# An order planned with table loads and GpSimd's hold counted, exponentials of blocks 4 to 7 from PSUM, weights' signs by a relu's slope

## The chip, the core and the metric

One core of one Trainium2 chip runs the whole program. The metric is the device time of one execution in microseconds, median of three runs: 699.13 us (697.25 to 700.21).

## What is computed

Sliding-window attention, then a gated MLP, then an MLP with a normalised hidden layer, all in float32:

```
scores = (q @ k.T) / 8, kept where 0 <= i - j < 64       # 4 batches, 8 heads, 576 positions, 64 wide
x  = softmax(scores) @ v                                  # heads side by side: 2304 tokens x 512
h  = x @ w_in;   g = h * tanh(softplus(h));   x2 = g @ w_out              # 512 -> 2048 -> 512
h  = x2 @ w_in2; y = h * softmax(h);  z = (y - mean) / sqrt(var + 1e-6) * g_ln
out = z @ w_out2                                          # 512 -> 1024 -> 512
```

The weights come as 64-bit floats and are read as pairs of 32-bit words.

## The kernel before

Every matmul of the MLPs runs on split operands: a value is rounded to its high part, the rest is its low part, and three products (low by high, high by low, high by high) are summed in PSUM.

**Blocks and groups.** The 2304 tokens are 36 blocks of 64, in five groups of 512, 512, 512, 384 and 384 tokens. Blocks 0 to 3 (`attend_first`) go one by one, all others in pairs (`attend`, n = 4, 6, ...). A block's chain is: scores on PE (`a_qk`, L610; for blocks 0 to 7 the mask is added by a matmul, L595, L602), maximum on VectorE (`a_max`, L657), subtraction (`a_sub`, L667 or L670), exponential on ScalarE, sum, reciprocal (`a_norm`, L686), multiplication by it on VectorE or POOL (`a_mul`, L693), transposes on PE (`a_tr`, L705), eviction (`a_pt`, L308), product with v (`a_pv`, L742), and x with its high part (`a_x`) and low part (`a_xl`, L764). The pairs' scores, transposes and products share one PSUM tile of pool `ps_a`. Exponentials come in three forms: head by head from PSUM for blocks 0 to 3 (`a_exp0`, L627), in one instruction after `a_sub` (`a_exp`, L674: blocks 4 to 7 and from 16 on), and head by head in SBUF (`a_exp1`, L641: blocks 8 to 15).

**The mish loop.** `its` lists 84 steps: group 0 in two halves of 256 tokens for features 0 to 3, then whole groups. A step is `pe_m1` (L788, 12 matmuls), mish on ScalarE (`act_m`, L798), the high part g on either engine (`g_h`), the low part on VectorE (`g_l`, L316), `pe_m2` (L822, 8 matmuls) and `pe_m2l` (L833, 4). The attention of a group runs beside the mish steps of the group ahead.

**Weights.** A piece is loaded by SP (`c_load`, L354), then `c_up` (upper word, scaled by 2^-112), `c_low` (lower word as an integer, scaled), `c_bits` (both joined, L377), `c_sign` (the sign bit of the upper word added, L383), and the high and low parts (`c_hi`, `c_lo`).

**The last stage** multiplies pairs of tiles by w_in2 in seven products (`b_p`, L957), sums them (`b_c`), normalises, transposes (`b_tr`, L1040), splits the result into lz (`b_hi`, `b_lo`), and multiplies by w_out2 (`b_m4`, L1065).

**What sets the order.** Each instruction belongs to a step with a cost for each engine that may run it, a due time and its predecessors. `Schedule.run` places the steps one after the other on the engines by these costs and the rings of buffers, and issues them in that order; each engine then runs its own queue in order. The due times come from the constants at the top (`ATT_AT`, `MISH_AT`, ...). Where the planner leaves PE idle for over 0.8 us, `bridge` fills part of the wait with zero matmuls of 256 columns (L562), and `warm_up` begins with `N_WARM` of them. ScalarE's functions need a table to be loaded (ACT_TABLE_LOAD) when it goes from exponentials to mish or back; the copy needs none. The planner charges each exponential of blocks 8 to 15 for a table load, whether one is needed or not:

```
ex = step(dict(act=1.68 + 1.33), t + offs[4], a_exp1, n, range(NP), after=[su], uses=[s])
```

Of the kernel before, what the change touches and what calls it, by code (L numbers as in the profile page):

```python
# [24 lines left out]
P = 128  # L25
BLK = 64
# [7 lines left out]
EARLY = 2  # L34
COSTS = {
    "up1": {"act": 0.58, "pool": 0.7}, "up2": {"act": 1.05}, "low1": {"pool": 0.83, "act": 0.58}, "low2": {"act": 1.05},
# [6 lines left out]
    "mul0": {"pool": 1.05, "dve": 0.69}, "mul": {"pool": 2.2, "dve": 1.23},  # L43
# [34 lines left out]
N_WARM = 42  # L78
# [3 lines left out]
W_AT = -57.813  # L82
# [8 lines left out]
class Schedule:  # L91
# [11 lines left out]
    def step(self, costs, due, fn, *args, after=(), new=(), uses=()):  # L103

        s = Step()
        s.costs, s.due, s.fn, s.args, s.after, s.new = costs, due, fn, args, list(after), new
        s.end = s.engine = None
        for b in uses:
            b["users"].append(s)
        self.steps.append(s)  # L110
        return s

    def issue(self, s, t):
        self.idle = s.idle if s.engine == "pe" else 0.0
        if any(s.costs is c for c in COSTS.values()):
            s.fn(s.engine, *s.args)
        else:
            s.fn(*s.args)

    def run(self, sizes):  # L120
# [8 lines left out]
        free = {e: 0.0 for s in self.steps for e in s.costs}  # L129
        ready = {e: [] for e in free}  # L130
# [35 lines left out]
        while left:  # L166
# [21 lines left out]
            s.end = t + s.costs[e]  # L188
# [15 lines left out]
def attention_moe_solu(  # L204
# [34 lines left out]
    NM = GROUPS[0] // BLK if PE_MASK else N0  # L239
    assert GROUPS[0] // BLK <= NBB  # L240
# [391 lines left out]


# [28 lines left out]
    def a_sub(n):  # L662
        s, nm = s_t[n]
        nm = nm.unsqueeze(2).to_broadcast([P, 2 * NP, P])
        if n < NM:
            ps, s = s, at_p.tile([P, 2 * NP, P], F32, tag="s2", name="s", bufs=2)
            nc.vector.scalar_tensor_tensor(out=s, in0=ps, scalar=scale, in1=nm, op0=ALU.mult, op1=ALU.add)  # L667
            s_t[n] = s, nm
        else:
# [810 lines left out]
```

## Time and profile before

| | |
|---|---|
| median of the runs | 699.13 us (697.25 to 700.21) |
| the profiled execution | 698.97 us, its span 697.2 us |
| PE | 680.7 us busy (98%), 4373 matmuls |
| VectorE | 398.3 us (57%), 689 instructions |
| ScalarE | 363.7 us (52%), 612 instructions, 35 of them table loads |
| POOL | 49.1 us (7%), 68 instructions |
| granted clock of PE | 0.999 |

The span runs from the first to the last instruction on the core; the time is that of the whole execution. Busy time of PE counts zero matmuls too. Shares over the whole span mix stages with different limits, so the rows below are cut by stage.

### The profile page before, as it was taken

How to read it: one execution, taken by the hardware profiler on the slowest of the kernel's cores; microseconds unless marked ns; L12 is line 12 of the kernel's file. 1: busy time of each engine (PE TensorE's matmuls, PEld its weight loads, DVE VectorE, ACT ScalarE, POOL GpSimd, SP SyncE). 2: the span in 40 equal slices, each digit the busy share in tenths (PEclk: the TensorE clock that was granted, in tenths of full speed). 3: DMA queues.
4: the chain of work that ended last, by engine and by line, in shares of the span. 5: the costliest groups of instructions: out<-in, count | busy, mean ns of one | idle time of the engine just before them, and what ended most of it. 6: DMA issues, size and time to landing. Idle time of an engine off the chain costs nothing.

```text
span 697.2 us, 10836 instructions
## 1 busy us (share of the span) xinstructions
PE 680.7 (98%) x4373; PEld 584.7 (84%) x4373; DVE 398.3 (57%) x689; ACT 363.7 (52%) x612; POOL 49.1 (7%) x68
## 2 busy tenths in 40 slices
PE   9979899999999999999999999999999999999997
PEld 7778778888887878888889999999778888888886
DVE  4897777788355557411344134764688777775430
ACT  4769975658245454422254223663567566555431
POOL 4121100000011111000010000000011101110000
PEclk9999999999999999999999999999999999999999
DMA  8857246487046324200023003320211111100011
GB/s 286 304 179 275 92 152 214 149 307 236 7 152 206 122 91 151 91 1 0 1 92 121 1 1 106 132 80 25 81 47 47 45 46 61 61 31 15 16 47 45
DMA packets 37858, 71.74 MB, mean 103 GB/s; under 512 B 2864, under 2 KB 15152, under 8 KB 37808
## 3 DMA queue, kind: packets, MB, share of 16 engines
q1 hardware_dynamic: 37808, 71.06, 30.1%
q8 instruction: 34, 0.56, 0.3%
q14 instruction: 16, 0.13, 0.1%
HBM read 59.51 MB, written 11.53 MB: 102 GB/s over the span
## 4 chain that ended last, share of the span: by engine, by line
PE 88%; ACT 6%; DVE 2%; DMA 1%; issue 1%; SPq 0%; POOL 0%; ACTq 0%; POOLq 0%
PE ps_h L788 26%; PE x L822 18%; PE po L1065 14%; PE pb L957 11%; PE x L833 9%; PE pt L1040 2%; PE ps_s L610 2%; PE ps_o L742 2%; PE ps_t L705 2%; DMA st<-w_out 1%; PE ps_w L562 1%; ACT s L641 1%; ACT L641 1%; ACT L798 1%; ACT st L362 1%
## 5 line engine op out<-in xcount | busy, mean ns | idle before, releaser
L788 PE MATMUL ps_h<-xt,w 128*128 128x512 f32 (+2 forms) x1008 | 211.6, 359 | 0.0
L788 PEld LDWEIGHTS ps_h<-xt,w 128*128 128x128 f32 x1008 | 177.9, 188 | 21.7 <-issue 0.5
L822 PE MATMUL x<-g,w 128*128 128x512 f32 (+2 forms) x672 | 147.7, 361 | 1.0 <-ACT g L296 1.0
L822 PEld LDWEIGHTS x<-g,w 128*128 128x128 f32 x672 | 118.0, 188 | 15.3 <-ACT g L296 1.2
L316 DVE SCALAR_TENSOR_TENSOR g<-mc,g 128x512 fp32r<-128x512 f32 (+2 forms) x84 | 53.4, 636 | 125.5 <-ACT g L296 124.6
L798 ACT ACTIVATE mc<-ps_h 128x512 f32<-128x512 f32 (+2 forms) x84 | 44.8, 536 | 133.9 <-PE ps_h L788 132.2
L1065 PE MATMUL po<-w,lz 128*128 128x512 f32 x432 | 100.5, 390 | 0.7 <-ACT lz L1046 0.7
L1065 PEld LDWEIGHTS po<-w,lz 128*128 128x128 f32 x432 | 80.7, 188 | 17.6 <-ACT lz L1046 0.9
L833 PE MATMUL x<-g,w 128*128 128x512 f32 (+2 forms) x336 | 82.0, 365 | 0.0
L833 PEld LDWEIGHTS x<-g,w 128*128 128x128 f32 x336 | 58.7, 188 | 7.7 <-issue 1.2
L957 PE MATMUL pb<-w,xs 128*128 128x512 f32 x210 | 50.9, 398 | 0.0
L296 ACT ACTIVATE g<-mc 128x512 fp32r<-128x512 f32 (+2 forms) x61 | 35.0, 576 | 28.0 <-PE x L833 26.8
L957 PEld LDWEIGHTS pb<-w,xs 128*128 128x128 f32 x210 | 38.9, 188 | 8.9
L693 POOL TENSOR_TENSOR s<-s,rs 128x1024 f32<-128x1024 f32 x11 | 20.9, 1898 | 317.5 <-DVE rs L687 306.5
L957 PE MATMUL pb<-w,xs_w 128*128 128x512 f32 x168 | 40.4, 394 | 0.6 <-ACT v_b L308 0.6
L308 ACT ACTIVATE v_b<-pb 128x512 f32<-128x512 f32 x34 | 20.2, 597 | 34.5 <-PE pb L957 34.5
L1050 DVE TENSOR_TENSOR lz<-pt,lz 128x512 fp32r<-128x512 f32 x36 | 23.4, 686 | 24.9 <-ACT lz L1046 24.9
L957 PEld LDWEIGHTS pb<-w,xs_w 128*128 128x128 f32 x168 | 31.0, 188 | 7.3 <-ACT v_b L308 1.1
L377 DVE SCALAR_TENSOR_TENSOR st<-st 128x1024 uint32<-128x1024 uint32 x22 | 26.9, 1223 | 9.4 <-ACT st L369 8.1
L798 ACT ACT_TABLE_LOAD x17 | 21.8, 1283 | 16.6 <-PE ps_h L788 16.4
L1020 POOL TENSOR_SCALAR va<-va 128x1 f32<-128x1 f32 x18 | 9.8, 546 | 289.1 <-DVE va L1013 289.1
L1072 ACT ACTIVATE o<-po 128x512 f32<-128x512 f32 x18 | 10.8, 601 | 35.7 <-PE po L1065 22.4
(130 smaller groups left out, 781.7 us busy)
## 6 DMA issues: line engine op xcount, KB each, us to landing
qk<-qk SPq DMA_DIRECT2D x32, 512.0 KB, 4.8
st<-w_out SPq DMA_DIRECT2D x12, 1024.0 KB, 5.4
st<-w_in SPq DMA_DIRECT2D x10, 1024.0 KB, 6.0
v<-v SPq DMA_DIRECT2D x32, 256.0 KB, 3.5
xr<-x2d SPq DMA_DIRECT2D x18, 256.0 KB, 3.3
out<-o SPq DMA_DIRECT2D x18, 256.0 KB, 2.0
x2d<-xs SPq DMA_DIRECT2D x12, 256.0 KB, 3.9
part<-xs SPq DMA_DIRECT2D x8, 256.0 KB, 3.6
```

What stands on the lines that cost most here:

```text
L296: nc.scalar.activation(out=hi, in_=x, func=ACTF.Copy, scale=1.0 if g is None else g)
L308: nc.scalar.activation(out=out, in_=x, func=ACTF.Copy)
L316: nc.vector.scalar_tensor_tensor(out=lo, in0=x, scalar=1.0 if g is None else g, in1=hi.bitcast(F32), op0=ALU.mult, op1=ALU.subtract)
L377: nc.vector.scalar_tensor_tensor(out=lw, in0=uw, scalar=3, in1=lw, op0=ALU.logical_shift_left, op1=ALU.bitwise_or)
L693: eng.tensor_tensor(out=s, in0=s, in1=rs.to_broadcast(list(s.shape)), op=ALU.mult)
L788: nc.tensor.matmul(out=ps[:, :n], lhsT=w[:, a, k, fs], rhs=x[:, b, k, a0:a1], start=(idx == 0), stop=(idx == len(terms) - 1),)
L798: nc.scalar.activation(out=c[:, :n], in_=ht.pop(i)[:, :n], func=ACTF.Mish)
L822: nc.tensor.matmul(out=acc[j][m][:, a0:a1], lhsT=w[:, a, f % 4, m * P:(m + 1) * P], rhs=g[:, 0, :n], start=(i in opens and a == 0), stop=F ...
L833: nc.tensor.matmul(out=acc[j][m][:, a0:a1], lhsT=w[:, 0, f % 4, m * P:(m + 1) * P], rhs=g[:, 1, :n], start=False, stop=i in closes,)
L957: nc.tensor.matmul(out=ps, lhsT=x[:, a, ix, k, :], rhs=w[:, k, :], start=first and n == 0, stop=n == len(terms) - 1, skip_group_check=not ...
L1050: nc.vector.tensor_tensor(out=lt[t][:, 1, fs], in0=pst[t][:, fs], in1=lt[t][:, 0, fs].bitcast(F32), op=ALU.subtract)
L1065: nc.tensor.matmul(out=po[t], lhsT=lz[:, a, f, :], rhs=wt["w4", f // 4][:, b, f % 4, :], start=(c == 0 and idx == 0), stop=(c == 2 and idx ...
```

## The change

The planner keeps the table that ScalarE has loaded, and adds 1.3 us where a step needs the other one; it holds VectorE back while a POOL instruction of two operands runs; it counts the first matmuls at half rate, and starts with the DMAs. The costs of the exponentials lose their fixed table load. All due times have new values, so nearly every queue has a new order.

Blocks 4 to 7 (`NM` stays 8) no longer run `a_sub`: the new `a_exp2` takes each head's exponential from PSUM with scale and bias, and sums it on the way. The PSUM tile is free only after the eighth.

Where ScalarE has the exponentials' table at `c_up`, it runs a Prelu with slope 2^32 for negative values in place of the copy, and `c_sign` is dropped for that piece. The exponentials' rows of blocks 0 to 3 get a room of their own, with four slots in place of three (`N_S`). `N_WARM` goes from 42 to 30.

```
-    "mul0": {"pool": 1.05, "dve": 0.69}, "mul": {"pool": 2.2, "dve": 1.23},
+    "mul0": {"pool": 1.05, "dve": 0.69}, "mul": {"pool": 1.9, "dve": 1.23},
...
-ATT_AT = (-49.865, -54.03, 11.767, 61.451, 29.509, -54.936, 25.627, -16.828, 25.86, -58.794, 5.065, -38.341)
+ATT_AT = (-86.017, -45.412, -6.323, 72.547, -11.313, 2.222, 41.979, -34.721, 27.367, -76.85, -34.655, -4.363)
...
-N_WARM = 42
+N_S = 4
+N_MASKED = 8
+N_WARM = 30
...
+            if e == "act" and s.table and s.table != self.table:
+                return max(t, free[e] + LOAD)
             return max(t, free[e])
...
-            s.end = t + s.costs[e]
+            cost = s.costs[e]
+            if e == "pe" and t < COLD:
+                cost += min(cost, (COLD - t) / 2)
+            if s.table and e == "act":
+                self.table = s.table
+            if s.sign is not None and e == "act" and self.table == "exp":
+                s.sign.costs = COSTS["no_sign"]
+            if s.two and e == "dve":
+                a, b = max(t, shared[0]), shared[1]
+                if a < b and t + cost > a:
+                    cost += min(b - a, (t + cost - a) / 0.2) * 0.8
+            if s.two and e == "pool":
+                shared = t, t + cost
+                b = min(free["dve"], t + cost)
+                if b > t:
+                    free["dve"] += 0.8 * (b - t)
+            s.end = t + cost
...
         if e == "act":
-            nc.scalar.activation(out=w, in_=w, func=ACTF.Copy, scale=2.0**-112)
+            if sch.table == "exp":
+
+                nc.scalar.activation(out=w, in_=w, func=ACTF.Prelu, scale=2.0**-112, alpha=2.0**32)
+            else:
+                nc.scalar.activation(out=w, in_=w, func=ACTF.Copy, scale=2.0**-112)
...
+    def a_exp2(n, ps):
+        if 0 in ps:
+            s = at_p.tile([P, 2 * NP, P], F32, tag="s2", name="s", bufs=2)
+            s_t[n] = s, s_t[n][1], sm_p.tile([P, 2 * NP], F32, tag="su2", name="su"), s_t[n][0]
+        s, nm, su, w = s_t[n]
+        for p in ps:
+            nc.scalar.activation(
+                out=s[:, p], in_=w[:, p], func=ACTF.Exp, scale=scale, bias=nm[:, p:p + 1], accum_out=su[:, p:p + 1]
+            )
+        if 2 * NP - 1 in ps:
+            s_t[n] = s, nm, su
...
-                su = step(dict(dve=1.23), t + offs[3], a_sub, n, after=[mx], new=[s], uses=[S, s, nm])
...
-            if NM <= n < N1:
+            if n < NM:
+                ex = step(dict(act=1.55), t + offs[4], a_exp2, n, range(NP), after=[mx], new=[s], uses=[S, s, nm], table="exp")
+                sm = step(dict(act=1.55), t + offs[4], a_exp2, n, range(NP, 2 * NP), after=[ex], uses=[S, s, nm], table="exp")
+            elif n < N1:
```

What moves, at three places. The first is SP's queue from its start: `room_kv` is k of blocks 0 to 3, `room_q` their q, `room_b` the first weights, `qk` the q and k of a later block. Before, then with the change:

```order
L354 DMA room_b<-w_in 128x4x256
L546 DMA room_kv<-k 128x4x128
L533 DMA room_q<-qk 128x512 x2
L546 DMA room_kv<-k 128x4x128
L354 DMA room_b<-w_in 128x4x256
```

```order
L579 DMA room_kv<-k 128x4x128
L382 DMA room_b<-w_in 128x4x256
L579 DMA room_kv<-k 128x4x128
L566 DMA room_q<-qk 128x512 x4
L544 DMA qk<-qk 128x1024 x2
```

The q of block 0 is issued fourth, not third, behind both pieces of k; the second piece of weights is behind all q.

The second is ScalarE's queue between the exponentials of block 10 and those of block 12 (`mc` is mish of `ps_h`, `xt` the high part of x, `s,su` the exponentials of a head, `st` a weight piece). Before, then with the change:

```order
L641 ACT_TABLE_LOAD
L641 ACTIVATE s,su<-s,nm 128x128 x4
L798 ACT_TABLE_LOAD
L798 ACTIVATE mc<-ps_h 128x256
L362 ACTIVATE st<-st 128x1024
L296 ACTIVATE g<-mc 128x256
L369 ACTIVATE st<-st 128x1024
L641 ACT_TABLE_LOAD
L641 ACTIVATE s,su<-s,nm 128x128 x4
```

```order
L686 ACT_TABLE_LOAD
L686 ACTIVATE s,su<-s,nm 128x128 x8
L838 ACT_TABLE_LOAD
L838 ACTIVATE mc<-ps_h 128x256
L394 ACTIVATE st<-st 128x1024
L401 ACTIVATE st<-st 128x1024
L838 ACTIVATE mc<-ps_h 128x512
L324 ACTIVATE g<-mc 128x256
L324 ACTIVATE g<-mc 128x512
L336 ACTIVATE s<-ps_t 128x512 x2
L686 ACT_TABLE_LOAD
```

Eight exponentials stand together, and two mish behind one load.

The third is VectorE's queue at block 14's normalisation (`rs` its reciprocal, L693 and L733 the multiplication). Before, then with the change:

```order
L764 TENSOR_TENSOR xt<-ps_o,xt 128x4x128
L377 SCALAR_TENSOR_TENSOR st<-st 128x1024
L383 SCALAR_TENSOR_TENSOR st<-st 128x1024
L686 TENSOR_SCALAR rs<-su 128x8
L687 RECIPROCAL rs<-rs 128x8
L693 TENSOR_TENSOR s<-s,rs 128x1024
```

```order
L409 SCALAR_TENSOR_TENSOR st<-st 128x1024
L417 SCALAR_TENSOR_TENSOR st<-st 128x1024
L804 TENSOR_TENSOR xt<-ps_o,xt 128x4x128
L726 TENSOR_SCALAR rs<-su 128x8
L727 RECIPROCAL rs<-rs 128x8
L733 TENSOR_TENSOR s<-s,rs 128x1024
```

The two weight steps have gone ahead of the x of block 12, and nothing stands between that and the normalisation.

## Rows read from the trace of the kernel before

**Rows 1.** Busy time by stage: stretch, its length, busy us (instructions) by engine, clock, DMA.

```profile
core 0: us, PE busy (x) PEld busy (x) DVE busy (x) ACT busy (x) POOL busy (x), PEclk, DMA share, GB/s
...
8.46:44.08 35.62, 30.64 (x394) 26.73 (x393) 30.33 (x51) 23.61 (x60) 8.22 (x7) 1.00 0.74 274
44.08:91.20 47.12, 43.56 (x461) 38.57 (x461) 35.18 (x46) 45.31 (x103) 5.69 (x3) 1.00 0.54 185
91.20:102.60 11.40, 10.05 (x74) 7.83 (x73) 8.45 (x12) 9.72 (x13) 0.00 (x0) 1.00 0.51 177
102.60:489.40 386.80, 386.80 (x2453) 339.65 (x2452) 194.63 (x251) 173.73 (x246) 11.39 (x6) 1.00 0.31 103
489.40:520.00 30.60, 28.84 (x132) 22.97 (x132) 21.77 (x57) 18.93 (x33) 2.32 (x4) 1.00 0.21 69
520.00:697.20 177.20, 173.38 (x825) 143.42 (x823) 106.35 (x274) 88.92 (x155) 17.81 (x32) 1.00 0.12 41
```

**Rows 2.** PE's timeline at the start: start, length, instruction, count [idle before].

```profile
1.04 7.58 PE L562 MATMUL ps_w<-warm 128*128 128x256 bf16 x42 [1.04 <-DVE warm L555]
8.46 0.39 PE L592 MATMUL ps_s<-room_kv,room_q 128*128 128x128 f32 x2
```

**Rows 3.** Busy time of the zero matmuls' line alone behind the first scores.

```profile
8.46:44.08 35.62, 7.90 (x62) 5.56 (x61) 1.00 0.74 274
```

**Rows 4.** SP's timeline: the issue of the first two q.

```profile
1.92 1.07 SPq L533 DMA_DIRECT2D room_q<-qk  x2
```

**Rows 5.** DMA issues from 1.9 and from 2.6 us: count, size, us to landing.

```profile
room_q<-qk SPq DMA_DIRECT2D x1, 256.0 KB, 5.0
...
room_q<-qk SPq DMA_DIRECT2D x1, 256.0 KB, 5.1
```

**Rows 6.** Timeline around one switch of ScalarE's table.

```profile
60.01 0.57 ACT L308 ACTIVATE xt<-ps_o 128x512 fp32r<-128x512 f32 x1
60.59 1.28 ACT L798 ACT_TABLE_LOAD   x1
...
61.89 0.39 ACT L798 ACTIVATE mc<-ps_h 128x256 f32<-128x256 f32 x1
```

**Rows 7.** ScalarE's groups, 44.08 to 91.20 us: count, busy us, mean ns, idle before.

```profile
L641 ACT ACT_TABLE_LOAD x6 | 7.7, 1283 | 0.1
L798 ACT ACT_TABLE_LOAD x5 | 6.4, 1283 | 0.5 <-PE ps_h L788 0.5
```

**Rows 8.** ScalarE's groups over the whole span.

```profile
L362 ACT ACTIVATE st<-st 128x1024 f32<-128x1024 f32 x22 | 25.3, 1149 | 6.3 <-DMA st<-w_in 4.3 <-DMA st<-w_out 1.9
...
L674 ACT ACTIVATE s<-s 128x1024 f32<-128x1024 f32 x12 | 12.7, 1060 | 0.1
L641 ACT ACTIVATE s<-s,nm 128x128 f32<-128x128 f32 x32 | 12.5, 391 | 0.1
```

**Rows 9.** VectorE's groups over the whole span, shapes apart.

```profile
L383 DVE SCALAR_TENSOR_TENSOR st<-st 128x1024 uint32<-128x1024 uint32 x22 | 27.0, 1225 | 0.5
...
L693 DVE TENSOR_TENSOR s<-s,rs 128x1024 f32<-128x1024 f32 x5 | 6.1, 1226 | 0.2
...
L667 DVE SCALAR_TENSOR_TENSOR s<-ps_s,nm 128x1024 f32<-128x1024 f32 x2 | 2.4, 1220 | 0.0
...
L383 DVE SCALAR_TENSOR_TENSOR room_b<-room_b 128x512 uint32<-128x512 uint32 x2 | 1.4, 696 | 0.0
```

**Rows 10.** Timeline of all engines, 36 to 42 us.

```profile
36.11 2.41 DVE L316 SCALAR_TENSOR_TENSOR g<-mc,g 128x256 fp32r<-128x256 f32 x2
36.34 1.90 POOL L693 TENSOR_TENSOR s<-s,rs 128x1024 f32<-128x1024 f32 x1 [7.35 <-DVE rs L687]
...
39.18 1.10 PE L610 MATMUL ps_s<-qk 64*64 64x128 f32 x32 [2.49 <-DVE xt L764]
...
41.59 0.41 DVE L316 SCALAR_TENSOR_TENSOR g<-mc,g 128x256 fp32r<-128x256 f32 x1
```

**Rows 11.** PE's timeline in the exit: block 14's transposes and the matmul behind.

```profile
94.56 1.07 PE L705 MATMUL ps_t<-ident,s 128*128 128x128 f32 x8 [0.35 <-DVE s L693]
96.63 2.11 PE L822 MATMUL x<-g,w 128*128 128x512 f32 x8 [1.00 <-ACT g L296]
```

More of the change, by code (lines that the diff above doesn't have):

```diff
@@ L98, in __init__, with step @@
         self.steps = []
+        self.table = "exp"
     def buf(self, ring):
         return dict(ring=ring, users=[])
-    def step(self, costs, due, fn, *args, after=(), new=(), uses=()):
+    def step(self, costs, due, fn, *args, after=(), new=(), uses=(), table=None, two=False):
         s = Step()
         s.costs, s.due, s.fn, s.args, s.after, s.new = costs, due, fn, args, list(after), new
-        s.end = s.engine = None
+        s.end = s.engine = s.sign = None
+        s.table, s.two = table, two
         for b in uses:
@@ L148, in start @@
         def start(s, e):
-            t = max([d.end + delay(d.engine, e) for d in s.after], default=0.0)
+            t = max([d.end + delay(d.engine, e) for d in s.after], default=-9.0)
             taken = {}
@@ L664, in a_sub @@
         nm = nm.unsqueeze(2).to_broadcast([P, 2 * NP, P])
[L665 to L669, printed above, removed]
-            nc.vector.tensor_tensor(out=s, in0=s, in1=nm, op=ALU.add)
+        nc.vector.tensor_tensor(out=s, in0=s, in1=nm, op=ALU.add)
     def a_exp(n):
@@ L1086, in attention_moe_solu @@
         room_q, room_kv, room_b = Buf("w1"), Buf("w2"), Buf("w2")
-        q0 = step(dict(none=0.0), -100, open_q0, new=[room_q], uses=[room_q])
+        room_s = Buf("w1")
+        q0 = step(dict(none=0.0), -100, open_q0, new=[room_q, room_s], uses=[room_q, room_s])
         mask0_r = step(dict(act=0.4), -99, make_mask_r, ((0, ident), (1, mask_0)), after=[mask0, q0], uses=[room_q])
@@ L1111, in convert @@
             o = CONV_PRIO
-            ld = step(dict(dma=1.4 * k), FIRST_AT[p["i"]] if p["i"] < len(FIRST_AT) else u + o[0], c_load, p, new=new, uses=[st], after=(first_ld[:1] if staged and p["i"] else []) + ([oe] if p["i"] in EXTRA else []))
+            ld = step(dict(dma=1.4 * k + (0.3 if k == 1 else 0.0)), FIRST_AT[p["i"]] if p["i"] < len(FIRST_AT) else u + o[0], c_load, p, new=new, uses=[st], after=(first_ld[:1] if staged and p["i"] else []) + ([oe] if p["i"] in EXTRA else []))
             first_ld.append(ld)
@@ L1115, in convert @@
             low = step(COSTS[f"low{k}"], u + o[1], c_low, p, after=[ld], uses=[st])
-            bits = step(COSTS[f"bits{k}"], u + o[2], c_bits, p, after=[up, low], uses=[st])
-            sign = step(COSTS[f"bits{k}"], u + o[3], c_sign, p, after=[bits], uses=[st])
+            bits = step(COSTS[f"bits{k}"], u + o[2], c_bits, p, after=[up, low], uses=[st], two=True)
+            sign = up.sign = step(COSTS[f"bits{k}"], u + o[3], c_sign, p, after=[bits], uses=[st], two=True)
             if nm == "w3":
@@ L1126, in convert @@
             first_hi.setdefault(key, [hi])
-            lo = step(COSTS[f"{g}_lo{k}"], u + o[5], c_lo, p, after=[hi], uses=[st])
+            lo = step(COSTS[f"{g}_lo{k}"], u + o[5], c_lo, p, after=[hi], uses=[st], two=True)
             for i in range(k):
@@ L1269, in mish @@
             )
-            c = step(dict(act=0.1 + 0.38 * k), o[1], act_m, i, after=[m1], new=[mc], uses=[h, mc])
+            c = step(dict(act=0.1 + 0.38 * k), o[1], act_m, i, after=[m1], new=[mc], uses=[h, mc], table="mish")
             gh = step(COSTS["g_hi" if a1 - a0 > 256 else "g_hi0"], o[2], g_h, i, after=[c], new=[g], uses=[mc, g])
-            gl = step(COSTS["g_lo" if a1 - a0 > 256 else "g_lo0"], o[3], g_l, i, after=[gh], uses=[mc, g])
+            gl = step(COSTS["g_lo" if a1 - a0 > 256 else "g_lo0"], o[3], g_l, i, after=[gh], uses=[mc, g], two=True)
             new = []
@@ L1406, in attention_moe_solu @@
             mx_ = step(dict(dve=0.22), o[0], b_max, t, after=[cs[t, 0], cs[t, 1]], new=[nm], uses=[h, nm])
-            ex = step(dict(act=1.23), o[1], b_exp, t, after=[mx_], new=[y, su], uses=[h, y, su, nm])
+            ex = step(dict(act=1.23), o[1], b_exp, t, after=[mx_], new=[y, su], uses=[h, y, su, nm], table="exp")
             sa = step(dict(dve=1.7), o[2], b_y, t, after=[ex], new=[st], uses=[h, y, su, st])
```

96 lines of the change are left out of this document (51 added, 45 removed).

## Prediction

> **What bounds the kernel now.** I read the stages first [rows 1]: the span cut where the work changes. From 102.60 to 489.40 us PE is busy for all of 386.80 us, and after 520.00 it stands still only for its last 3.8 us (177.20 less 173.38), the eviction and store of the last tile. There the matmuls themselves are the bound, and no order of the other engines makes them shorter. PE is short of work in three places. Until 8.46 us it runs 42 zero matmuls ahead of the first scores [rows 2]. From 8.46 to 102.60 it is idle for 5.0 + 3.6 + 1.4 us, and fills a further 7.9 us with the zero matmuls that `bridge` puts into waits the planner foresaw [rows 3]. At the entry of the last stage, 489.40 to 520.00, it idles 1.8 us [rows 1]. So some 18 us behind the first scores, 8.5 ahead of them and 1.8 later are not work, out of 697.2.
>
> Who keeps PE waiting differs by stage [rows 1]. From 8.46 to 44.08 VectorE is busy 30.3 of 35.6 us. From 44.08 (the table load ahead of block 8's exponentials) to 91.20 (the last exponential of block 14) ScalarE is busy 45.3 of 47.1 us: there it is the bound, and eleven table loads of 1.283 us lie in it [rows 7]. In the exit, 91.20 to 102.60, a chain decides: two weight steps on VectorE, behind them block 14's normalisation, its transposes, and a matmul that waits 1.00 us for ScalarE's g [rows 11].
>
> **The parts of the change** are counted against the profiled execution: span 697.2 us and 1.8 us around it (698.97), 0.16 us under the median of 699.13.
>
> *Start.* Twelve zero matmuls go, but the first scores also need their q. It closes the first 1,024 KB of the queue and landed at 1.92 + 5.0 = 6.9 us; the next 256 KB landed some 0.6 us later, at about 2.46 + 5.1 = 7.5 us [rows 4, 5]. On the new SP queue this q has one more piece of 256 KB ahead of it, so I take 7.5 us, and 0.1 to begin: **-0.9 us** (ends 0, and -1.5 if q lands as before).
>
> *Blocks 0 to 7, up to block 8's table load.* The exponentials of blocks 4 to 7 run from PSUM, head by head: twice 8 x 0.391 = 3.1 us on ScalarE in place of 1.06 us, +4.1 us [rows 8]. VectorE loses two subtractions and two sums (four instructions of about 1.22 us, -4.9) and two signs, one of 0.70 and one of 1.23 us (-1.9). It takes five multiplications from POOL, three of them of half size: 2 x 1.23 + 3 x 0.70 = +4.5 us [rows 9]. POOL's hold goes with them: two g rests took 2.41 us while a POOL multiplication of 1.90 us ran, and 0.41 is what one of them takes alone [rows 10], so -1.6 us. VectorE: -4.9 - 1.9 + 4.5 - 1.6 = -3.9. In this stage PE, VectorE and ScalarE work one behind the other through the one tile of pool ps_a, so +4.1 and -3.9 meet in series and nearly cancel. A wait is added: block 6's scores stand on PE until ps_a is released, now by block 4's eighth exponential; behind them in PE's queue are block 3's `a_pv` and the first two `pe_m1`. For it, these two come ahead of block 4's transposes. Step by step block 8's table load comes to 42.8 instead of 44.08: **-1.3 us with the start, so -0.4 beyond it** (ends +4.1 and -3.9).
>
> *Blocks 8 to 15, the ScalarE stage.* In the order of the change seven table loads stand from block 8's to block 14's exponentials, not eleven. In the trace a switch costs its load and nothing beside it: an eviction ends at 60.58, the load runs from 60.59, the mish from 61.89 [rows 6]. Four fewer: -5.1 us. The Trainium skill's page "ScalarE: Activation LUTs", section "What ACT_TABLE_LOAD costs", puts a drain of about 1.38 us beside the same load, 2.66 us a switch; by it the four would give -10.6 us. This trace shows no such gap, and the row decides. The rest of ScalarE's work in the stage keeps its size, so 47.1 - 5.1 = 42.0 us if it waits as little as before (1.8 us). With PE no longer starved by it, it waits more for PE: around block 8's x, block 10's scores and the first full-width mish I put 2.6 us. So 44.6 in place of 47.1 us: **-2.5 us** (ends 0, where it waits as long as it saved, and -5.1). VectorE is no worse off: three multiplications of 1.23 us come from POOL, and signs of 1.225 us leave where the relu's slope does their work [rows 9].
>
> *Exit to group 2's first `pe_m1`.* It took 11.4 us, with one `pe_m2l` still owed behind it: half of the eight matmuls that take 2.11 us [rows 11], about 1.0. In the new order the normalisation stands right behind block 12's x: the transposes come 1.8 us after the last exponential, not 3.4 (94.56 - 91.20), -1.6. The `pe_m2` that waited for g is now ahead of the transposes, -1.0 for the wait and -2.0 for its own time, and the owed 1.0 is done. Against it ScalarE has two weight steps of 1.15 us [rows 8] ahead of block 14's x, of which PE's work covers 0.6, so the first `pe_m1` waits 1.7 us for x. Sum: -1.6 - 1.0 - 2.0 - 1.0 + 1.7 = **-3.9 us** (ends -5.6 without that wait, and 0).
>
> *102.60 to 489.40.* The orders of all engines change and PE's work doesn't; VectorE and ScalarE are busy about half of it [rows 1]: 0.
>
> *Entry of the last stage.* PE's new order fills the wait for the first normalised tile with 24 matmuls of the third pair. The wait from transposes to lz stays, so of 1.8 us idle I take **-1.1 us** (ends -1.8, and +1.1 if the third pair's operands are late).
>
> *Nothing:* the DMAs moved on SP behind the start (two w_out pieces go ahead of the q and k of blocks 8 and 9, and land while ScalarE is still with block 6), the fourth slot of `room_s`, the planner's own code.
>
> Sum: -1.3 - 2.5 - 3.9 - 1.1 = -8.8 us; span 688.4, and with 1.8 us around it **690.2 us**.
>
> **The rivals.**
>
> *Not passed on.* The first stages get shorter, but weights, g or x are then late by as much in the mish loop, or each turn through ps_a takes as long as before. For it: the same weight conversions lie in fewer microseconds. Against: 386.8 us of PE without a visible wait, with half of the other engines free [rows 1]. What is left is the start and the entry, -2.0: 697 us.
>
> *PE's clock falls*, the one that ends on the other side. The zero matmuls behind the first scores go from 69 to 45 (counted in the two orders), and PE waits for block 8's and block 10's scores without any. If the granted clock goes to 1.2 GHz there, each us of matmul work costs one more; with 15 us of work at that level the sum is -8.8 + 15 = +6.2: 705 us. It decides from 12.3 us on (8.8 and the 3.5 of half a per cent). Against: PE idled 2.49 us ahead of block 8's scores [rows 10], and the granted clock of that stage is 1.00, the 2.4 GHz level [rows 1]. The Trainium skill's page "TensorE: Matmul & The Clock Gate", section "What's actually happening", says that the low clock is the default and that idling brings it back; by that rule fewer zero matmuls speak against this change, and this trace has no fall to show.
>
> *The relu with a slope costs more than the copy.* No row shows it. The nearest is the copy of the same shape, 1.15 us, which I took, with the exponential at 1.06 [rows 8]; at twice the copy, five and a half of them up to block 14's last exponential give +6.3 us on ScalarE: 696.5 us.
>
> *All waits vanish.* The low ends of the ScalarE stage, the exit and the entry: -1.3 - 5.1 - 5.6 - 1.8 = -13.8: 685.2 us.
>
> **How the numbers follow.** The forecast, a gain between 4 and 12 us, gets 0.68; the full gain 0.06; not passed on 0.15; the dear relu 0.04; the clock 0.07. About 0.5% (3.5 us) is what a measurement of this kernel can tell from no change. Faster, under 695.6, are the forecast and the full gain: 0.74. Slower, over 702.6, is the clock's: 0.07. The rest is 0.19. The range reaches from the full gain, 685.2, to the cases that keep little more than the start, 698.
>
> **What would show it.** First scores near 7.6 us; 31 table loads in place of 35, seven of them between block 8's and block 14's exponentials; that stretch 44 to 45 us with ScalarE over 94% busy; group 2's first `pe_m1` near 96, and PE never idle from there to the last stage; granted clock 1.00 throughout; relu rows near 1.15 us. Wrong would be: that `pe_m1` later than 100, PE idle between 110 and 480, or a slice with the clock under 1.

## The result, and the profile after

The changed kernel takes **691.30 us**, median of four runs (690.54 to 692.19), beside 699.06 for the kernel before: ratio 0.9892 (95% interval 0.9867 to 0.9916), a gain of 1.1%. The forecast was 690.2. The profiled execution has a span of 690.3 us. The same kernel was profiled once more beside the last experiments (`e12_same`, below): span 688.9. The two differ only ahead of block 8's table load, so the steps are checked against both.

Busy time by stage of the changed kernel, first profile, cut at the same marks as [rows 1]:

```profile
core 0: us, PE busy (x) PEld busy (x) DVE busy (x) ACT busy (x) POOL busy (x), PEclk, DMA share, GB/s
8.51:45.49 36.98, 32.91 (x393) 28.80 (x394) 29.00 (x56) 26.87 (x90) 0.65 (x1) 0.95 0.74 274
45.49:89.28 43.79, 42.91 (x445) 37.55 (x444) 38.92 (x49) 41.87 (x103) 0.00 (x0) 1.00 0.62 212
89.28:97.85 8.57, 8.57 (x70) 6.66 (x68) 5.83 (x9) 7.48 (x12) 0.00 (x0) 1.00 0.74 250
97.85:483.92 386.07, 386.07 (x2449) 338.99 (x2449) 191.48 (x244) 175.48 (x249) 4.57 (x2) 1.00 0.30 101
483.92:514.60 30.68, 29.99 (x138) 24.21 (x138) 23.43 (x62) 20.28 (x35) 2.09 (x4) 1.00 0.19 61
514.60:690.30 175.70, 171.91 (x819) 142.48 (x817) 106.04 (x272) 85.11 (x150) 15.96 (x32) 1.00 0.13 43
```

The first three rows of the second profile of the same kernel:

```profile
core 0: us, PE busy (x) PEld busy (x) DVE busy (x) ACT busy (x) POOL busy (x), PEclk, DMA share, GB/s
8.55:44.10 35.55, 31.68 (x393) 27.48 (x394) 28.95 (x56) 27.21 (x90) 0.65 (x1) 1.00 0.77 284
44.10:87.89 43.79, 42.91 (x445) 37.56 (x444) 38.91 (x49) 41.94 (x103) 0.00 (x0) 1.00 0.61 213
87.89:96.46 8.57, 8.57 (x70) 6.67 (x68) 5.83 (x9) 7.48 (x12) 0.00 (x0) 1.00 0.65 246
```

Set beside the prediction's terms (stretches in us; the ScalarE stage runs to the end of block 14's last exponential, the exit to group 2's first `pe_m1`; the predicted column is the prediction's own marks):

| | before | predicted | first profile | second |
|---|---|---|---|---|
| first scores begin at | 8.46 | 7.6 | 8.51 | 8.55 |
| block 8's table load at | 44.08 | 42.8 | 45.49 | 44.10 |
| ScalarE stage | 47.1 | 44.6 | 43.79 | 43.79 |
| exit | 11.4, and 1.0 owed | 8.5 | 8.57 | 8.57 |
| to the last stage | 386.8, the 1.0 in it | 385.8 | 386.07 | 386.03 |
| last stage to the end | 207.8 | 206.7 | 206.38 | 206.41 |
| span | 697.2 | 688.4 | 690.3 | 688.9 |

From block 8's table load on, every term came to within a microsecond. The one ahead of it did not: no gain where the clock holds, and a loss of 1.4 us in the first profile. There the granted clock is 0.95, the only stage under 1. PE's timeline and two stretches of the first profile show where:

```profile
8.51 0.76 PE L625 MATMUL ps_s<-room_kv,room_q 128*128 128x128 f32 x2 [2.08 <-DMA room_q<-qk]
```

```profile
8.00:10.00 2.00, 1.49 (x7) 1.40 (x8) 0.69 (x1) 0.14 (x1) 0.00 (x0) 0.62 1.06 419
10.00:12.00 2.00, 2.00 (x12) 1.81 (x12) 0.66 (x1) 0.00 (x0) 0.00 (x0) 0.53 1.02 395
```

The 30 zero matmuls end at 6.43 us, PE waits 2.08 us for q, and the first scores then run at the 1.2 GHz level until 11.7: 12 matmuls between 10 and 12 us, 22 in the second profile:

```profile
10.00:12.00 2.00, 2.00 (x22) 1.95 (x20) 1.43 (x3) 0.90 (x5) 0.00 (x0) 1.00 1.01 395
```

In the ScalarE stage, its groups in the first profile (count, busy us, mean ns, idle before) answer to [rows 7, 8]:

```profile
L686 ACT ACT_TABLE_LOAD x4 | 5.1, 1283 | 0.1
L838 ACT ACT_TABLE_LOAD x3 | 3.8, 1283 | 0.1
L394 ACT ACTIVATE st<-st 128x1024 f32<-128x1024 f32 x3 | 3.5, 1165 | 1.2 <-DMA st<-w_in 1.2
...
L392 ACT ACTIVATE st<-st 128x1024 f32<-128x1024 f32 x2 | 2.3, 1128 | 0.0
```

Seven loads, as forecast (31 over the span, 35 before), and the Prelu (L392) costs no more than the copy (L394) does.

### The profile page after: what moved, and what is told of

The parts are those of the page before. It is cut to its first block, busy times and chain, and to the rows that moved or that the text cites. A ratio compares the mean times of both kernels' runs of the same rounds, so it can differ in the third digit from the quotient of the medians.

```text
span 690.3 us, 10742 instructions
## 1 busy us (share of the span) xinstructions
PE 677.8 (98%) x4337; PEld 582.6 (84%) x4337; DVE 395.9 (57%) x690; ACT 360.5 (52%) x638; POOL 27.0 (4%) x55
## 4 chain that ended last, share of the span: by engine, by line
PE 95%; DMA 2%; ACT 1%; DVE 1%; SPq 0%; issue 0%; ACTq 0%
PE ps_h L828 28%; PE x L862 19%; PE po L1105 14%; PE pb L997 13%; PE x L873 10%; PE ps_o L782 2%; PE pt L1080 2%; PE ps_s L643 2%; PE ps_t L745 2%; DMA room_b<-w_in 1%; PE ps_s L625 1%; DMA room_q<-qk 1%; ACT s L673 0%; PE ps_o L595 0%; DVE w L344 0%; SPq L579 0%
## 5 line engine op out<-in xcount | busy, mean ns | idle before, releaser
L344 DVE SCALAR_TENSOR_TENSOR g<-mc,g 128x512 fp32r<-128x512 f32 (+2 forms) x84 | 51.9, 620 | 116.8 <-ACT g L324 115.7
L1105 PE MATMUL po<-w,lz 128*128 128x512 f32 x432 | 102.5, 392 | 0.7 <-ACT lz L1086 0.7
L324 ACT ACTIVATE g<-mc 128x512 fp32r<-128x512 f32 (+2 forms) x67 | 38.7, 580 | 11.9 <-PE x L873 10.2
L997 PE MATMUL pb<-w,xs_w 128*128 128x512 f32 x168 | 40.2, 392 | 0.0
L336 ACT ACTIVATE v_b<-pb 128x512 f32<-128x512 f32 x31 | 18.4, 598 | 30.6 <-PE pb L997 26.2
L1029 ACT ACTIVATE e<-h_b,nm 128x1024 f32<-128x1024 f32 x18 | 20.7, 1151 | 14.2 <-DVE nm L1020 14.2
L1012 DVE CUSTOM_DVE_ANT_0 h_b<-pb,v_b 128x512 f32<-128x512 f32 x27 | 18.2, 687 | 16.5 <-PE pt L1080 10.2
L1036 DVE CUSTOM_DVE_ANT_0 h_b<-h_b,e 128x1024 f32<-128x1024 f32 x18 | 22.0, 1221 | 9.1 <-ACT e L1029 9.1
```

What stands on the lines that cost most here:

```text
L324: nc.scalar.activation(out=hi, in_=x, func=ACTF.Copy, scale=1.0 if g is None else g)
L344: nc.vector.scalar_tensor_tensor(out=lo, in0=x, scalar=1.0 if g is None else g, in1=hi.bitcast(F32), op0=ALU.mult, op1=ALU.subtract)
L997: nc.tensor.matmul(out=ps, lhsT=x[:, a, ix, k, :], rhs=w[:, k, :], start=first and n == 0, stop=n == len(terms) - 1, skip_group_check=not ...
L1029: nc.scalar.activation(out=e, in_=h2[t], func=ACTF.Exp, bias=nrm[t], accum_out=su)
L1036: nc.vector.tensor_tensor_reduce(out=y, in0=y, in1=e, scale=1.0, scalar=0.0, op0=ALU.mult, op1=ALU.add, accum_out=st[:, :1])
L1105: nc.tensor.matmul(out=po[t], lhsT=lz[:, a, f, :], rhs=wt["w4", f // 4][:, b, f % 4, :], start=(c == 0 and idx == 0), stop=(c == 2 and idx ...
```

## The experiments

Each keeps the changed kernel's order but for the edit. For that, the steps are first collected in the order in which the planner places them, and then issued from that list, in which an edit can move one:

```
     def issue(self, s, t):
+        self.queue.append((s, t, self.table))
+
+    def emit(self, s, t, table):
...
+        q = self.queue
...
+        for s, t, table in q:
+            self.emit(s, t, table)
```

All times at a glance (median of 4 or 5 runs; ratio to the kernel before in the same runs, 95%). Only `e9` to `e11` ran beside the unchanged kernel, `e12_same`; the times of the others are compared with it by their ratios. Stretches and span are those of the profiled execution:

| run | us | ratio | block 8's load | ScalarE stage | exit | span |
|---|---|---|---|---|---|---|
| e12_same | 690.76 | 0.9889 (0.9868 to 0.9910) | 44.10 | 43.79 | 8.57 | 688.9 |
| e1_warm50 | 692.29 | 0.9887 (0.9873 to 0.9902) | 43.91 | 45.51 | 8.91 | 690.7 |
| e2_q_second | 690.68 | 0.9874 (0.9850 to 0.9897) | 43.64 | 43.79 | 8.57 | 688.4 |
| e3_w_in_ahead | 691.03 | 0.9871 (0.9856 to 0.9886) | 43.96 | 43.79 | 8.57 | 688.9 |
| e4_q_and_w_in | 690.49 | 0.9860 (0.9844 to 0.9877) | 43.44 | 45.05 | 8.85 | 690.1 |
| e5_loads | 696.27 | 0.9958 (0.9940 to 0.9976) | 44.16 | 49.07 | 8.60 | 694.2 |
| e6_sub | 693.20 | 0.9921 (0.9891 to 0.9952) | 48.90 | 44.26 | 9.62 | 695.1 |
| e7_signs | 694.76 | 0.9928 (0.9908 to 0.9948) | 45.57 | 45.74 | 9.39 | 693.0 |
| e8_pool | 692.07 | 0.9894 (0.9868 to 0.9921) | 43.92 | 44.56 | 8.63 | 690.4 |
| e9_weights_first | 692.52 | 0.9918 (0.9892 to 0.9944) | 43.83 | 44.40 | 9.86 | 690.7 |
| e10_no_late_zeros | 691.44 | 0.9901 (0.9873 to 0.9928) | 43.06 | 44.75 | 8.77 | 688.9 |
| e11_three | 688.94 | 0.9862 (0.9842 to 0.9881) | 41.70 | 45.16 | 8.71 | 687.9 |

### The start: warm-up, q, the third weights

`e1_warm50`:

```
-        zeros(ps_h.tile([P, 512], F32, tag="h", name="ps_w"), N_WARM)
+        zeros(ps_h.tile([P, 512], F32, tag="h", name="ps_w"), 50)
```

> The changed kernel with 50 zero matmuls at the start in place of 30, all else in its order. In its trace PE stops at 6.43 us, waits 2.08 us for block 0's q, and the granted clock is 0.50 from 8.5 to about 11.7 us. Clock theory: the wait itself brings the clock down; 20 more zero matmuls cover it, the first scores still begin near 8.5 us but at clock 1.00, the scores of block 3 end 1.6 us earlier (14.5 in place of 16.14), and block 8's table load comes at 43.9 in place of 45.49: about 689.7 us. Rival, the third piece of weights: it lands at 27.36 whatever the first scores do, so block 8's table load stays within 0.5 us of 45.49 and the time at 691.3. Second rival: the clock falls for another reason, and stays at 0.50 behind 8.5 us with 50 as with 30.

`e2_q_second`, `e3_w_in_ahead` (`e4_q_and_w_in` has both):

```
+        x = q.pop(at(*('open_q0',)))
+        q.insert(at(*('load_k0', 0)), x)
+        x = q.pop(at(*('load_q0', 0)))
+        q.insert(at(*('c_load', ('w1', 0))), x)
```

```
+        x = q.pop(at(*('c_load', ('w1', 2))))
+        q.insert(at(*('load_qk', 6)), x)
```

(`open_q0` only sets up the room that this q is loaded into.)

> The changed kernel with block 0's q issued second on SP, behind the first piece of k and ahead of the first weights and of the second piece of k. Theory: the first scores wait for the bytes ahead of their q, 1,024 KB with the change; with 256 KB ahead (the first 512 KB had landed at 4.42 us in the trace of before) q lands at 4.5 to 5.5 us, PE goes from its 30 zero matmuls (end 6.43) to the scores with no gap and keeps clock 1.00. The first scores begin at 6.5 in place of 8.51, those of block 3 end up to 3.6 us earlier, and block 8's table load comes at 41.9 to 42.5: 687.7 to 688.3 us. Rival, the third piece of weights lands near 27 all the same: table load 45 and 691 us.

> The changed kernel with the third piece of weights (1,024 KB of w_in) issued ahead of block 6's q and k, which wait on SP for block 4's scores to free their slot; in the order before the change it stood ahead of them too. Theory: its landing at 27.36 is a wait of 1.74 us on ScalarE, on whose queue block 3's x stands behind it and with that group 0's first pe_m1. Issued near 10 us it lands near 18, the 1.74 us go, the first pe_m1 begins at 28.6 in place of 30.36, and block 8's table load comes at 43.8 in place of 45.49: 689.6 us. Rival: blocks 4 and 6 turn through the one tile of ps_a behind it at their own pace, so the first pe_m1 is earlier but block 8's table load less than 0.5 us: 691 us. The other way: block 6's q and k land 2.7 us later behind it and its scores with them: 692 to 693 us.

> Both moves on SP together. If the two waits are separate steps of one chain, their gains add: block 8's table load at 45.49 - 3.6 - 1.7 = 40.2, and 686.0 us. If the later one absorbs the earlier, the time is that of the better of the two alone.

With 50 zero matmuls the clock is 1.00 and the load comes at 43.91, as the clock theory said; the time does not follow, since the ScalarE stage then waits 2.36 us for a piece of w_out (last section). But the second profile of the unchanged order waits longer ahead of its first scores, and its clock does not fall:

```profile
8.55 0.46 PE L625 MATMUL ps_s<-room_kv,room_q 128*128 128x128 f32 x2 [2.79 <-DMA room_q<-qk]
```

So the wait is not enough to bring the clock down; it falls behind such a wait in some executions. What a fall costs here is read from one pair of profiles of one kernel, as `e12_same` (below) expected: 45.49 - 44.10 = 1.4 us, all of it kept to the end (690.3 and 688.9). That covering the wait prevents a fall is not shown, since it did not fall without cover either in most runs.

q second on SP brings the first scores to 6.45 us as expected, 2 us earlier, and the load to 43.64: 0.3 to 0.5 of the 2 us arrive. The next block waits instead:

```profile
9.01 0.49 PE L639 MATMUL ps_s<-room_kv,room_q 128*128 128x128 f32 x2 [1.12 <-DMA room_q<-qk]
```

These are block 1's scores, waiting for block 1's q. From them to block 8's table load it is 34 to 35 us in each of these runs. The third weights: ScalarE's wait for them, 1.74 us in the first profile and 0.70 in the second, is gone in `e3_w_in_ahead`, and the load stays at 43.96, 0.14 ahead of 44.10, where the rival had it: ScalarE runs ahead, and waits later in the same chain. Together the two give 43.44. My estimate of 40.2 summed waits that lie beside one another. None of the three times differs from that of the unchanged kernel beyond the intervals.

### Four table loads more

`e5_loads`:

```
+        nc.gpsimd.memset(tiny, 0.0)
...
+    tiny = const.tile([P, 2], F32, name="tiny")
...
     def act_m(i):
+        if i in (5, 8, 40, 50, 60, 70):
+            nc.scalar.activation(out=tiny[:, 1:], in_=tiny[:, :1], func=ACTF.Exp)
```

> The changed kernel with an exponential of one column put ahead of six mish, each costing a table load to and one back: two of the six in the ScalarE stage (ahead of the mish of steps 5 and 8), so four loads, the number that the change took away, and four in the mish loop (steps 40, 50, 60, 70), eight loads. Theory: in the stage ScalarE is the bound, so the four loads lengthen the stretch from block 8's table load to block 14's last exponential from 43.9 us by 4 x 1.283 and two small exponentials of some 0.2 us, to 49 to 49.5 us, and the time by as much, to 696.5 us or so; the eight in the loop (10.3 us of ScalarE) lengthen nothing, and the stretch from group 2's first pe_m1 to the last stage stays at 386.2 us. Rival, the stage has slack: it grows by under 2.6 us and the time is under 694. Second rival, a switch costs more than its load (a drain beside it): the stage grows by 8 us or more.

The stage and the loop, and the loads in the stage:

```profile
44.16:93.23 49.07, 44.74 (x445) 39.07 (x444) 38.92 (x49) 47.66 (x108) 0.00 (x0) 0.97 0.58 192
93.23:101.83 8.60, 8.60 (x71) 6.67 (x69) 5.83 (x9) 7.49 (x12) 0.00 (x0) 1.00 0.70 238
101.83:488.04 386.21, 386.21 (x2450) 338.98 (x2449) 191.48 (x244) 183.76 (x259) 4.57 (x2) 1.00 0.31 101
```

```profile
L849 ACT ACT_TABLE_LOAD x5 | 6.4, 1283 | 0.1
L694 ACT ACT_TABLE_LOAD x4 | 5.1, 1283 | 0.1
L846 ACT ACT_TABLE_LOAD x2 | 2.6, 1283 | 0.0
...
L846 ACT ACTIVATE tiny<-tiny 128x1 f32<-128x1 f32 x2 | 0.4, 203 | 0.0
```

Eleven loads again, and the stage is 49.07 - 43.79 = 5.28 us longer: nearly all of the four loads (5.13) and two exponentials of 0.20 us. The clock fell in this stage too, to a mean of 0.97, but ScalarE's idle time in it is 1.41 us, against 1.92 without the loads, so the fall did not lengthen it; the one execution at clock 1.0 has a span of 693.7, 4.8 us over 688.9. In the loop six loads came in, not the eight of the expectation (41 over the span in place of 31). With four exponentials they keep ScalarE busy 8 us more, and lengthen the loop by 0.2 of 386 us. That is the theory in both halves: a load counts nearly in full in the stage that ScalarE bounds, and next to nothing in the loop, where PE never waits. Both rivals are out. The Trainium skill's page "ScalarE: Activation LUTs", section "What ACT_TABLE_LOAD costs", would have put 10.6 us on these four; this run gives 1.2 to 1.3 each.

### The parts undone one by one

`e6_sub` (one subtraction, one exponential and one sum per pair again):

```
     def a_exp2(n, ps):
+        if 0 in ps:
+            w, nm = s_t[n]
+            s = at_p.tile([P, 2 * NP, P], F32, tag="s2", name="s", bufs=2)
+            nc.vector.scalar_tensor_tensor(
+                out=s, in0=w, scalar=scale, in1=nm.unsqueeze(2).to_broadcast([P, 2 * NP, P]), op0=ALU.mult, op1=ALU.add
+            )
+            nc.scalar.activation(out=s, in_=s, func=ACTF.Exp)
+            s_t[n] = s, None
+        else:
+            a_sum(n)
+        return
```

> The changed kernel with a_exp2 undone for blocks 4 to 7, all else in its order: one subtraction and one sum of 1.22 us each per pair on VectorE again, and one exponential of 1.06 us in place of eight of 0.39. ScalarE -4.1 us, VectorE +4.9 us ahead of block 8's table load, which comes at 43.9 us with the change where the clock holds. In the new order VectorE has hardly a gap from 14 to 44 us (2.6 us in all in the run with the third weights ahead). Theory: VectorE paces these blocks, so the load comes 3 to 5 us later, at 47 to 49, and the time is 694 to 696. Rival, as the prediction had it: the two meet in series and cancel, the load stays within 1 us of 43.9 and the time near 691. Second rival: ScalarE paces, the load comes at 40 and the time is 687.

`e7_signs`:

```
-            if sch.table == "exp":
+            if False:
...
-        if e != "none":
+        if True:
```

> The changed kernel with the copy in place of the Prelu at every c_up and the sign step back on VectorE where the change dropped it, all else in its order: eight sign instructions more, three ahead of block 8's table load (0.70 + 1.23 + 1.23 = 3.2 us), three in the ScalarE stage, the rest in the loop. Theory: VectorE paces the first blocks, so the load comes 2 to 3 us later than 43.9, and in the ScalarE stage the signs fall into VectorE's gaps, so that stretch stays at 43.9 us: 693 to 694 us. Rival: the signs fall beside waits everywhere, 691 us. Second rival: they delay the weights on which PE waits in the ScalarE stage too, 696 us or more. ScalarE's rows of the copy, against those of the Prelu, show what the slope costs: 0 by the theory.

`e8_pool`:

```
-        eng = nc.gpsimd if e == "pool" else nc.vector
+        eng = nc.gpsimd if e == "pool" or n in (0, 1, 2, 4, 6, 8, 10, 12) else nc.vector
```

> The changed kernel with the eight multiplications on POOL that were there before the change (blocks 0, 1, 2, 4, 6, 8, 10, 12), all else in its order. Each chain is longer by 1.04 - 0.69 or 1.90 - 1.23 us, VectorE loses 3 x 0.69 + 2 x 1.23 = 4.5 us ahead of block 8's table load, but is held while POOL works (3 x 1.04 + 2 x 1.90 = 6.9 us at most). Theory: the hold gives back about what VectorE saves, and the longer chains make the load 1 to 2 us later than 43.9; in the ScalarE stage nothing: 692 to 693 us. Rival: VectorE's saving counts more than the hold, the load comes 2 us earlier and the time is 689. Second rival: hold and chains add up through the whole stage, 696 us.

The profiled execution of `e6_sub` has two falls of the clock, at 8.5 and at 32 us, and its load at 48.90 can't be read without them. Its other three executions, at clock 1.0, have spans of 691.2 to 691.5, against 688.7 to 690.1 for the seven of the changed kernel at 0.999 or 1.000: undoing costs some 2 us (2.0 to 2.2 by the ratios, 0.9921 against 0.9892 and 0.9889), with intervals that overlap. That is half of what the theory of a pacing VectorE gives, and more than the 0.8 us (4.9 less 4.1) of a cancellation in series. How much of it lies ahead of block 8's load is not shown: these three have no trace, and in the traced one the stage and the exit behind the load are 0.5 and 1.0 us longer as well.

`e7_signs` costs 2.5 to 2.7 us by the ratios (0.9928 against 0.9892 and 0.9889), 4.1 between the profiled spans (693.0 and 688.9). Of 3.2 us of signs ahead of block 8's load 1.5 arrive (45.57 against 44.10). In the ScalarE stage the three signs fill no gaps, they make one:

```profile
56.73 1.15 ACT L400 ACTIVATE st<-st 128x1024 f32<-128x1024 f32 x1 [2.39 <-DVE st L415]
```

The stage is 2 us longer and VectorE busy 41.98 of its 45.74 us. The `st` pool has two slots, and the next piece is loaded only when VectorE is done with an earlier one. SP's issue of this piece, in this run and in the second profile of the changed kernel:

```profile
50.16 0.38 SPq L389 DMA_DIRECT2D st<-w_in  x1
```

```profile
47.42 0.38 SPq L382 DMA_DIRECT2D st<-w_in  x1
```

That is 4.59 us behind block 8's load in place of 3.32, one sign later. The piece lands 6.5 us behind its issue in both, here at 56.66: it is this landing that ScalarE's copy at 56.73 waits for, though the row names VectorE's L415, which ended at the same moment. The copies of this run take 1146 ns (L400, 22 of them), the Prelu of the first profile 1167 (L392, six over the span) and its copies 1147 (L394): the slope costs at most 0.02 us.

`e8_pool` brings the load 0.2 us earlier (43.92), makes the stage 0.8 us longer and moves the ratio by 0.0002 to 0.0005 (0.9894): POOL's hold and its longer multiplication, the case for moving them, are worth under 1 us in this order as far as intervals of some 2 us can tell.

### The exit

`e9_weights_first`:

```
+        a = [q.pop(at(*k)) for k in (("c_bits", ("w1", 9)), ("c_sign", ("w1", 9)))]
+        i = at("a_xl", 12)
+        q[i + 1:i + 1] = a
```

> The changed kernel with VectorE's two steps of a weight piece (1.22 us each) put back between the x of block 12 and block 14's normalisation, as they stood before the change; all else in its order. Theory: the normalisation comes some 1.5 to 2 us later, block 14's transposes 3.7 us behind the last exponential in place of 2.1, and the stretch from that exponential to group 2's first pe_m1 is 10.2 to 11.3 us in place of 8.57; the stage ahead of it stays at 43.8 us: the time 1.6 to 2.7 us longer, 693 to 694. Rival: pe_m1 waits for ScalarE's x of block 14 anyway, the exit stays within 0.5 us of 8.57 and the time within 0.5 us of the changed kernel's in the same runs.

PE's timeline in the exit, first of the changed kernel, then of this run, answers to [rows 11]:

```profile
91.56 1.04 PE L745 MATMUL ps_t<-ident,s 128*128 128x128 f32 x8
92.35 1.17 PE L873 MATMUL x<-g,w 128*128 128x512 f32 x4
93.36 1.99 PE L862 MATMUL x<-g,w 128*128 128x512 f32 x8
95.28 1.15 PE L782 MATMUL ps_o<-s,v 128*64 128x64 f32 x32
96.36 1.19 PE L873 MATMUL x<-g,w 128*128 128x512 f32 x4
97.39 0.50 PE L595 MATMUL ps_h<-warm 128*128 128x256 bf16 x3
```

```profile
91.62 1.06 PE L758 MATMUL ps_t<-ident,s 128*128 128x128 f32 x8 [0.95 <-DVE s L746]
```

With the two weight steps in front, the transposes begin 3.4 us behind the last exponential in place of 2.3, PE waits 0.95 us for the normalisation, and the exit is 9.86 us, 1.3 longer, a little under the theory's 1.6. The stage ahead of it is 0.6 us longer (44.40), where the theory had it unchanged; ScalarE waits 1.00 us for a piece of w_out in it. The time is 692.52 against 690.76 for the unchanged kernel in the same runs, so the rival's 0.5 is out.

### Zero matmuls that come too late, and all three together

`e10_no_late_zeros` (`e11_three` adds the two moves on SP):

```
-        if sch.idle > 0.8:
+        if sch.idle > 0.8 and not (sch.fn in ("a_qk", "a_pv") and sch.t < 45.0):
```

> The changed kernel without the 23 zero matmuls that stand ahead of a scores or a product step in the first 45 us (7, 5 and 11), all else in its order. In its trace these do not run in the wait that they were put in for: they write to the PSUM tile whose release is the wait, start when it ends, and hold the real matmuls back by 0.8, 0.5 and 1.36 us. Theory: block 4's product comes 1.4 to 1.9 us earlier, block 8's table load at 42.0 to 42.5 in place of 43.9 (where the clock holds), and the time is 1.4 to 1.9 us shorter. Rival: VectorE paces these blocks, the load stays within 0.5 us of 43.9. The other way: PE has more idle time, the granted clock falls behind it, and the load comes at 45 or later.

> The changed kernel with block 0's q second on SP, the third weights ahead of block 6's q and k, and without those 23 zero matmuls. If the gains add: block 8's table load at 43.4 - 1.4 to 1.9 = 41.5 to 42.0 and the time 2 us or more under the changed kernel's in the same runs, 688.5 to 689. Rival: one of the chains absorbs the others, as it did for q and weights together, and the time is within 1 us of the changed kernel's.

> The changed kernel itself, beside the others on the same chip. By the clock theory an execution in which PE's wait for the first q does not bring the clock down has block 8's table load at 43.9, not 45.49, and a span 1.6 us shorter than the 690.3 of the first profile: 688.7. Where the clock falls as it did there, 690.3.

`bridge` writes its zeros into the tile of the step that it stands before. Where PE waits for that tile to come free, they run behind the wait. PE's timeline of the changed kernel (second profile), then of `e10_no_late_zeros`, at block 4's product:

```profile
34.32 1.36 PE L595 MATMUL ps_o<-warm 128*128 128x256 bf16 x11 [1.23 <-ACT s L336]
35.61 1.15 PE L782 MATMUL ps_o<-s,v 128*64 128x64 f32 x32
```

```profile
33.81 1.15 PE L789 MATMUL ps_o<-s,v 128*64 128x64 f32 x32 [1.39 <-ACT s L343]
```

Without them block 4's product begins 1.8 us earlier, the load comes at 43.06, 1.0 earlier than 44.10 (1.4 to 1.9 were expected), and the time does not move: 691.44 against 690.76. The microsecond goes back in the ScalarE stage, 44.75 us in place of 43.79, which waits 1.51 us for a piece of w_out. `e11_three` has the load at 41.70, as expected, waits 2.03 us for the same transfer, and still ends at 688.94: each of its four times (688.82 to 689.77) is below every one of the changed kernel's in the same runs (690.55 to 692.02). It beats the kernel before by 1.4% and the changed one by 0.3%; of the latter the intervals of the two ratios overlap.

## Why the prediction was right, and where it was not

**Right in sum: 690.2 forecast, 691.3 measured** (690.76 in the second set). Part of that is luck: the 1.3 us forecast ahead of block 8's load did not come, and the ScalarE stage gave 0.8 us more than forecast. Shown by runs are the table loads, the signs, and 1.3 us of the exit; the rest of the exit and the end of the span are read off the traces, and no run undoes them. Step by step:

*Start.* Forecast -0.9; measured 0. q landed at 8.4 us, not 7.5: I took the 0.6 us by which the next 256 KB followed in [rows 5], where the trace of the change shows the fourth transfer 5.69 us behind its issue at 2.68. The rest of the error was in what an earlier start is worth: `e2_q_second` starts 2 us earlier and keeps 0.3 to 0.5 of it. So an earlier start, -0.9 or the low end's -1.5, would not have reached block 8's load in full either.

*Blocks 0 to 7.* Forecast -0.4; measured about 0 where the clock holds, against the term's ends of +4.1 and -3.9. The net came out close, **but its working is the step that failed**: I priced what the diff adds to and takes from VectorE (-3.9 us), and not what the new order moves onto it. VectorE's groups of the changed kernel up to block 8's load:

```profile
L338 DVE COPY room_s<-ps_t 128x512 f32<-128x512 f32 x2 | 1.4, 688 | 0.1
...
L344 DVE SCALAR_TENSOR_TENSOR w<-st,w 128x1024 fp32r<-128x1024 f32 x1 | 1.2, 1215 | 0.0
...
L328 DVE CAST w<-st 128x1024 fp32r<-128x1024 f32 x1 | 0.7, 696 | 0.0
...
L328 DVE CAST g<-mc 128x256 fp32r<-128x256 f32 x2 | 0.6, 294 | 0.7 <-PE x L873 0.5
```

One of the two copies, the split of a w_out piece (two rows) and both g casts, 0.7 + 1.2 + 0.7 + 0.6 = 3.2 us, were not VectorE's in that stretch before. Its busy time went from 30.33 to 29.00, not to 26.4. No run moves these instructions back, so what they cost the stretch is argued, not shown; of the 3.2 us of signs that `e7_signs` puts on VectorE there, 1.5 arrive. A second item is the zero matmuls that run behind the wait (1.0 us in `e10_no_late_zeros`); I had counted those of [rows 3] as filling waits (they end at 44.08; nine more, 1.1 us, follow at once). And "meet in series and nearly cancel" does not hold for the parts: undone, the exponentials cost some 2 us, and the signs ahead of the load 1.5.

*ScalarE stage.* Forecast -2.5, measured -3.3. The table loads are shown: put back, four of them with their two small exponentials cost 5.3 us. The waits put against them (2.6) were too many by 0.8. The term named the signs as neutral here; `e7_signs` shows 2 us. So the stage stands at 43.79 only because signs left VectorE as well.

*Exit.* Forecast -3.9. Exit and loop together give -3.6 (11.40 - 8.57 = 2.8, and 0.7 to 0.8 in the loop, where the owed `pe_m2l` was). The sum held, its parts less: the transposes come 2.3 us behind the last exponential, not 1.8; `pe_m1` does not wait 1.7 us for x, since a `pe_m2` and two `pe_m2l` stand in the exit and cover it but for three zero matmuls. The place of the weight steps, which I priced at 1.6, is 1.3 in `e9_weights_first`.

*Loop and last stage.* Forecast 0 and -1.1; PE is never idle in the loop, and the end is 1.4 us shorter: PE's idle time at the entry went from 1.8 to 0.7 us, as forecast, and 0.3 us is work.

*"Nothing: the DMAs moved on SP"* was right in the time and wrong in the reason: the third weights of w_in, now behind q and k that wait for a slot, made ScalarE wait 1.74 us (0.70 in the second profile); `e3_w_in_ahead` shows that this wait was covered.

*The rivals.* Not passed on: no, each stage kept its gain. The dear relu: no. **The clock** came true in kind, not in place or size: not for want of zero matmuls between block 8's and block 10's scores, but behind the wait ahead of the first ones, 1.4 us of it, in the profiled one of the first four executions (mean clock 0.998; the others, not traced, 0.999 or 1.000). I had read the 2.49 us of idle time in [rows 10] as proof that such a wait leaves the clock alone. The Trainium skill's page "TensorE: Matmul & The Clock Gate", section "What's actually happening", by which idling brings the low clock back, agrees in kind with the executions where it fell. Why the others kept the high clock no run here shows.

## What to carry to other kernels

Price a new order engine by engine from the full list of what stands in a stretch before and after, not from the operations that the diff adds and removes: work moved in took back most of VectorE's 3.9 us here. Count a table load in full where ScalarE bounds the stage, and as nothing where PE has work without a gap. A filler ahead of a wait must not need what the wait is for.

## What the runs showed of the hardware

The granted clock fell to 0.50 behind idle waits of PE of 1.85 us (`e6_sub`, first scores), 2.08 (first profile), 2.24 (`e5_loads`, at 59 us) and 2.54 (`e6_sub`, at 32 us), and stayed at 1.00 behind 2.27 (`e3_w_in_ahead`), 2.35 (`e5_loads`, first scores), 2.49 [rows 10] and 2.79 (`e12_same`): the length of the wait does not decide it alone. It is part of the spread between executions, for the kernel before too: of its executions beside the experiments, those with a mean clock of 0.999 or 1.000 have spans of 695.7 to 697.2 us, the others (0.993 to 0.998) 696.1 to 699.5. The changed kernel's seven at 0.999 or 1.000 have 688.7 to 690.1, and the one at 0.998 has 690.3: like with like the gain is still 7 to 8 us, so it is not the clock's.

A transfer's rate varies also. ScalarE waits for the same piece of w_out in seven of the profiles (0.2 to 2.4 us) and not at all in the others, `e12_same` and the first profile among them. Two stretches with the DMA engines fully busy, `e1_warm50` and then the first profile (the last two columns are DMA share and GB/s), and the wait that followed in the former:

```profile
62.00:64.00 2.00, 2.00 (x16) 1.87 (x16) 1.97 (x2) 1.98 (x7) 0.00 (x0) 1.00 1.02 281
```

```profile
64.00:66.00 2.00, 2.00 (x14) 1.79 (x13) 1.97 (x2) 1.97 (x6) 0.00 (x0) 1.00 1.03 420
```

```profile
66.93 1.16 ACT L401 ACTIVATE st<-st 128x1024 f32<-128x1024 f32 x1 [2.36 <-DMA st<-w_out]
```

The same share moves two thirds of the bytes, and the piece of w_out lands 8.3 us behind its issue in the former and 6.5 in the latter. What makes it so was not tried; this wait is what takes back the microsecond of `e10_no_late_zeros`, and the next one to remove.
